# First x blocks on a second DMA queue, the first four layer norms cut between units, and key features joined later

## The chip, the cores and the metric

The kernel runs on one core of one Trainium2 chip. The metric is the device time of one execution in microseconds (us), as the median of several executions. Profiles come from one execution each; "span" is the profiled time, about 1.7 to 1.9 us shorter than the metric of the same execution.

## The reference

Two layers, each used twice on x of 2048 x 1024 in bf16: linear attention with 32 heads, and a gated ReGLU block with inner width 3584. Layer norm stands before each.

```python
    def _A_ref(x, wqkv, wo):
        ...                                  # q, k, v = x @ wqkv, 32 heads of 32
        phi = lambda t: jnp.where(t > 0, t + 1, jnp.exp(t)) + 1e-6
        pq, pk = phi(q), phi(k)
        kv = jnp.einsum("bhsd,bhse->bhde", pk, v)
        ...                                  # num / den, then @ wo
    x = A_x
    x = x + _A_ref(_layernorm(x, axis=-1), A_wqkv, A_wo)
    x = x + _B_ref(_layernorm(x, axis=-1), B_W_gate, B_W_up, B_W_down)
    ...                                      # the same two once more
```

## The kernel before

x is kept as 16 blocks of 128 rows. In the first attention layer, a *unit* is one block times 512 columns of a weight: eight matmuls of 128x512 into one of four PSUM buffers. A key unit (columns k0 or k1) then goes through `phi`: ACT takes the Exp, DVE clamps it (`min` 1, plus 1e-6), and DVE joins it with max(x, 0) and so gives the PSUM buffer back. `later.at(n, f)` runs f after n further units. In the head (the first quarter of layer 0) the program fixes the order of DVE and ACT itself. In the kernel before it does so in two separate lists, the norms of blocks 0 to 3 and the units; in the changed kernel both stand in one list.

```python
    def head(self):
        ...                                  # 10 matmuls on a zero block, to warm TensorE up
        self.load_x(0, 0)                    # all on SyncE's queue
        self.load_x(0, 1)
        k0(0, H)
        self.load_x(1)
        k0(H, 2 * H)
        self.load_x(2)
        k1()
        self.load_x(3)
        ...
            for j in range(QT):              # blocks 0 to 3, one after the other
                for c in range(2):
                    self.ln_stat(j, src[j], c, stats[j])
                r = self.ln_rstd(stats[j])
                xn = self.xn_home(0, j)
                for h in (0, 1) if j == 0 else (None,):
                    self.ln_scale(src[j], *r, xn, h)
                for h in range(2):
                    turn(j, xn, h)           # 4 transposes, then a copy out of PSUM

    def phi(self, ps, out, kind):
        e = self.ep.tile([P, NW], F32, tag="e")
        if kind == "v":
            nc.scalar.activation(out=e, in_=ps, func=ACT.Exp)
            nc.vector.tensor_scalar(out=e, in0=e, scalar1=1.0, scalar2=1e-6, op0=ALU.min,
                                    op1=ALU.add)           # the clamp
        ...
        def join():
            nc.vector.scalar_tensor_tensor(out=out, in0=ps, scalar=0.0, in1=e,
                                           op0=ALU.max, op1=ALU.add)
        if self.phi_lag:                     # 2 in the head
            self.later.at(self.phi_lag, join)
```

Of the kernel before, what the change touches and what calls it, by code (L numbers as in the profile page):

```python
# [7 lines left out]
ALU = mybir.AluOpType  # L8
ACT = mybir.ActivationFunctionType
# [3 lines left out]
P = 128  # L13
NW = 512
HD = 32
QT = 4
LNLAG = 1
ZR = 5
NZ = 11
Z3 = 3  # L20
PHILAG = 2
KINDS = (("vvss", "vvss"), ("vvss", "vvss"))


class _Ring:
# [59 lines left out]
class _Net:  # L85
# [135 lines left out]
    def head(self):  # L221

        nc, tc, ring = self.nc, self.tc, self.ring
        H = self.KT // 2

        zero = self.ep.tile([P, NW], BF16, tag="e")
        nc.vector.memset(zero, 0.0)
        idle = self.ps3.tile([P, NW], F32, tag="b")
        for _ in range(10):
            nc.tensor.matmul(idle, lhsT=zero[:, 0:P], rhs=zero, start=True, stop=True)  # L230

        k0, k1, v0, q0, q1 = (ring.place() for _ in range(5))
        self.load_x(0, 0)
        self.load_x(0, 1)
        k0(0, H)
        self.load_x(1)
        k0(H, 2 * H)
        self.load_x(2)
        k1()
        self.load_x(3)  # L240
        q0()
        self.load_x(4)
        self.load_x(5)
        self.load_x(6)
        self.load_x(7)
        q1()
        for t in range(8, self.ST):
            self.load_x(t)
        v0()
        src = self.xb  # L250
        self.xnT[0, 0] = self.xnTp.tile([P, self.KT, QT * P], BF16, tag="xnT", name="xnT0_0")
        stats = [self.small.tile([P, 2, nc.vector.BN_STATS_DIM], F32, tag="stats", name=f"st{j}")
                 for j in range(QT)]

        def turn(j, xn, h):
            tp = self.ps3.tile([P, H, P], BF16, tag="b")
            for i in range(H):
                kt = h * H + i
                nc.tensor.transpose(tp[:, i, :], xn[:, kt * P:(kt + 1) * P], self.ident)
            dst = self.xnT[0, 0][:, h * H:(h + 1) * H, j * P:(j + 1) * P]  # L260
            if h == 0:
                nc.vector.tensor_copy(out=dst, in_=tp)
            else:
                nc.scalar.activation(out=dst, in_=tp, func=ACT.Copy)

        with tc.manual_schedule(engines={mybir.EngineType.DVE, mybir.EngineType.Activation}):
            for j in range(QT):
                for c in range(2):
                    self.ln_stat(j, src[j], c, stats[j])
                r = self.ln_rstd(stats[j])  # L270
                xn = self.xn_home(0, j)
                for h in (0, 1) if j == 0 else (None,):
                    self.ln_scale(src[j], *r, xn, h)
                for h in range(2):
                    turn(j, xn, h)

    def ln_turn(self, layer, t, xn):
        nc = self.nc
# [6 lines left out]
    def ln_at(self, delay, layer, t, lag):  # L285
        def stat():
            scale = self.ln_norm(layer, t)
            self.later.at(LNLAG, lambda: norm(scale))

        def norm(scale):  # L290
            xn = scale()
            self.later.at(lag, lambda: self.ln_turn(layer, t, xn))

        self.later.at(delay, stat)
# [5 lines left out]
    def phi(self, ps, out, kind):  # L300

        nc = self.nc
        e = self.ep.tile([P, NW], F32, tag="e")
        if kind == "v":
            nc.scalar.activation(out=e, in_=ps, func=ACT.Exp)
            nc.vector.tensor_scalar(out=e, in0=e, scalar1=1.0, scalar2=1e-6, op0=ALU.min,  # L306
                                    op1=ALU.add)
        else:
            nc.scalar.activation(out=e, in_=ps, func=ACT.Relu, scale=-1.0)
            nc.scalar.activation(out=e, in_=e, func=ACT.Exp, scale=-1.0)  # L310
            if kind == "s":
                nc.scalar.activation(out=e, in_=e, func=ACT.Identity, bias=self.eps6[:, 0:1])  # L312
            else:
                nc.gpsimd.tensor_tensor(out=e, in0=e, in1=self.eps6[:, 0:1].to_broadcast([P, NW]),
                                        op=ALU.add)
        def join():
            nc.vector.scalar_tensor_tensor(out=out, in0=ps, scalar=0.0, in1=e,  # L317
                                           op0=ALU.max, op1=ALU.add)

        if self.phi_lag:  # L320
            self.later.at(self.phi_lag, join)
        else:
            join()

    def load_x(self, t, c=None):
        D = self.D
        lo, hi = (0, D) if c is None else (c * D // 2, (c + 1) * D // 2)
        self.nc.sync.dma_start(out=self.xb[t][:, lo:hi], in_=self.x_v[:, t, lo:hi])


    def plan_A(self, l):
# [9 lines left out]
    def layer_A(self, l, last_ln):  # L341
        nc, G, KT, D = self.nc, self.G, self.KT, self.D
        ring, later = self.ring, self.later
# [5 lines left out]
        zrow = self.kvc.tile([P, D], BF16, tag="zrow")  # L349
        ksum = self.prodp.tile([P, D], F32, tag="prod", name=f"ksum{l}")  # L350

        def project(name, l_q, j):
            w = ring.get((l, name))
            ps = self.ps.tile([P, NW], F32, tag="a")
            for kt in range(KT):
                nc.tensor.matmul(ps, lhsT=self.xnT[l, l_q][:, kt, j * P:(j + 1) * P],  # L356
                                 rhs=w[:, kt, :], start=(kt == 0), stop=(kt == KT - 1))
            return ps

        def k_unit(q, j, c):  # L360
            t = q * QT + j
            pk = self.pk_home(l, t)
            self.phi(project(f"k{c}", q, j), pk[:, c * NW:(c + 1) * NW], KINDS[l // 2][min(q, 1)][c])
            later.at(1 + (10 if self.phi_lag else 0), lambda: k_sum(t, slice(c * NW, (c + 1) * NW)))

        def k_sum(t, cols):
# [54 lines left out]
        def q_unit(sc, j, c, lag=None):  # L421
            if c == 0 and (sc, j) not in pq_of:
                if sc < self.NQ - 1:
                    a = self.xnTp.tile([P, QT, D], BF16, tag="xnT", name=f"pq{l}_{sc}")
                    for i in range(QT):
                        pq_of[sc, i] = a[:, i, :]
                else:
                    pq_of[sc, j] = self.xnp.tile([P, D], BF16, tag="xn", name=f"pq{l}_{sc}_{j}")
            pq = pq_of[sc, j]
            self.phi(project(f"q{c}", sc, j), pq[:, c * NW:(c + 1) * NW], KINDS[l // 2][min(sc, 1)][2 + c] if sc < 3 else "v")  # L430
            if c == H - 1 and lag is not None:
                later.at(lag, lambda: z_mult(sc, j))

# [50 lines left out]
        def column_major(f, q):  # L484
            return [lambda j=j, c=c: f(q, j, c) for c in range(H) for j in range(QT)]
# [11 lines left out]
                        later.tick()  # L497

        if l == 0:
            self.head()  # L500
        else:
            ring.free_before((l, "k0"))
        for i in range(QT, self.ST):
            self.ln_at((4 if l == 0 else 2) + 3 * (i - QT), l, i, 2)
        first = column_major(k_unit, 0)
        if l == 0:

            first = [first[c * QT + j] for c, j in ((0, 0), (0, 1), (1, 0), (0, 2), (1, 1), (1, 2),
                                                    (0, 3), (1, 3))]

        def quarter0():
            self.phi_lag = PHILAG if l == 0 else 0
            run(first)
            run(column_major(q_unit, 0))
            later.at(1, lambda: None)
            self.phi_lag = 0
# [9 lines left out]
        run(row_major(k_unit, self.NQ - 1))  # L526
        with self.tc.manual_schedule(engines={mybir.EngineType.DVE, mybir.EngineType.Pool}):
            ring.free_before((l, "v0"))
            later.at(ZR, z_row)
            for i in range(NZ):  # L530
                later.at(ZR + 2 + 2 * i, lambda i=i: z_mult(*divmod(i, QT)))
            for d in range(KT):
                m_units(d)
            if l > 0:
                later.at(1, lambda: [self.bring_back(t) for t in range(self.NS)])
            q3 = row_major(q_unit, self.NQ - 1)
            out0 = column_major(out_unit, 0)

            def with_fold(u, i):
                return lambda: (u(), fold_wo(2 * i), fold_wo(2 * i + 1))  # L540

            run(q3[:3])
            run([with_fold(u, i) for i, u in enumerate(q3[3:] + out0[:3])])
            ring.free_slowly((l, "o0"), later, 2)
            for i in range(NZ, self.ST):
                later.at(1 + Z3 * (i - NZ), lambda i=i: z_mult(*divmod(i, QT)))
            run(out0[3:])
            self.ln_later(last_ln, 0, 5, 4, 3)
            for sc in range(1, self.NQ):
                run(row_major(out_unit, sc))  # L550
# [132 lines left out]
```

## Time and profile before

| | before |
|---|---|
| median of 4 executions | 1635.45 us (1635.25 to 1636.06) |
| profiled span | 1634.0 us |
| PE idle in the first 44.6 us | 6.6 us |
| second half of k0 / k1 landed (completion records) | 8.98 / 12.66 us |

This is the view of groups by shape, limited to 10 to 32 us; after the count come busy time, mean ns of one, and idle time of the engine just before it with its releaser.

```profile
L306 DVE TENSOR_SCALAR e<-e 128x512 f32<-128x512 f32 x8 | 5.9, 733 | 2.6 <-ACT e L305 2.5
```

For 2.5 us DVE stood in front of a clamp whose Exp was not ready. The longest of these waits, 1.47 us, stands ahead of a copy of transposed x whose transposes had ended at 10.49 us, and PE waits for that copy until 11.53:

```profile
10.71 0.43 DVE L306 TENSOR_SCALAR e<-e 128x512 f32<-128x512 f32 x1 [1.47 <-ACT e L305]
11.05 0.42 DVE L262 COPY xnT<-tp 128x512 bf16<-128x512 bf16 x1
```

### The profile page before, as it was taken

To read this page: it belongs to the slowest core of one execution; us is meant where nothing else is said; L and a number is where in the kernel's file an instruction comes from. 1 tells how busy PE (TensorE), PEld (TensorE's weight loads), DVE (VectorE), ACT (ScalarE), POOL (GpSimd) and SP (SyncE) were. 2 spreads that over 40 slices of the span, in tenths; PEclk is the share of its full clock that TensorE was granted. 3 is DMA by queue.
4 is the path that set the end of the run, shared out by engine and by line. 5 is a ranking of instruction groups with operands and counts; after the bars stand their busy time and mean duration, and the time that the engine had idled before them with its cause. 6 is when DMAs were issued, how large, how long until landed. Compare 5 with 4: busy or idle time off the path is not lost.

```text
span 1634.0 us, 18308 instructions
## 1 busy us (share of the span) xinstructions
PE 1616.6 (99%) x7506; PEld 742.7 (45%) x7658; DVE 571.6 (35%) x947; ACT 331.9 (20%) x635; POOL 201.8 (12%) x134
## 2 busy tenths in 40 slices
PE   8999999999999999999999999999999999999999
PEld 3444444444444444444444444444444444444444
DVE  7855585223112321222165547941122111211211
ACT  5841202101110110111067312121011101101110
POOL 2349230000000000000023592100000000000000
PEclk9999999999999999999999999999999999999999
DMA  8313547458445544444550147474554454454452
GB/s 251 59 52 52 174 74 188 146 165 232 154 139 175 175 151 158 160 150 141 168 129 1 52 91 251 79 198 145 177 162 149 156 191 155 145 162 157 155 161 72
DMA packets 298245, 235.05 MB, mean 144 GB/s; under 512 B 101296, under 2 KB 294192, under 8 KB 298160
## 3 DMA queue, kind: packets, MB, share of 16 engines
q1 hardware_dynamic: 293408, 229.66, 47.3%
q10 hardware_dynamic: 4752, 4.20, 0.8%
q8 instruction: 60, 0.98, 0.2%
q14 instruction: 25, 0.20, 0.0%
HBM read 201.33 MB, written 8.39 MB: 128 GB/s over the span
## 4 chain that ended last, share of the span: by engine, by line
PE 97%; DVE 1%; ACT 1%; issue 1%; DMA 0%; SPq 0%
PE pu L582 24%; PE pg L582 24%; PE acc L606 23%; PE ps L356 12%; PE ps L473 7%; PE ps L390 7%; PE kv L403 0%; PE fold L461 0%; DMA t<-in_A_wqkv_dram 0%; PE acc_last L606 0%; DVE e L306 0%; DVE stats L148 0%; DVE slab L317 0%; ACT e L310 0%; DVE st L148 0%
## 5 line engine op out<-in xcount | busy, mean ns | idle before, releaser
L582 PEld LDWEIGHTS <-t 128*128 128x128 bf16 x3584 | 350.7, 98 | 422.9
L582 PE MATMUL pu<-xnT,t 128*128 128x512 bf16 x1757 | 420.2, 379 | 1.9
L582 PE MATMUL pg<-xnT,t 128*128 128x512 bf16 x1756 | 419.8, 379 | 1.8
L606 PE MATMUL acc<-t,hT 128*128 128x512 bf16 x1727 | 380.6, 379 | 1.9
L588 DVE TENSOR_TENSOR hT<-pu,rg 128x512 bf16<-128x512 f32 x224 | 154.7, 691 | 572.8 <-PE pu L582 553.4
L587 ACT ACTIVATE rg<-pg 128x512 f32<-128x512 f32 x224 | 133.5, 596 | 737.3 <-PE pg L582 665.9
L606 PEld LDWEIGHTS <-hT 128*128 128x128 bf16 x1820 | 178.1, 98 | 209.0
L356 PE MATMUL ps<-t,xnT 128*128 128x512 bf16 x1002 | 223.3, 379 | 5.5 <-DVE slab L317 1.4
L356 PEld LDWEIGHTS <-xnT 128*128 128x128 bf16 x1024 | 99.8, 98 | 125.1 <-issue 4.7
L473 PE MATMUL ps<-T,pqT 128*128 128x512 bf16 x502 | 111.3, 379 | 0.5
L155 ACT ACTIVATE rstd<-mv,eps 128x1 f32<-128x1 f32 x64 | 18.8, 294 | 333.3 <-DVE mv L153 333.3
L623 DVE TENSOR_TENSOR xo<-x,acc 128x512 bf16<-128x512 f32 x31 | 21.3, 687 | 170.3 <-PE acc L606 170.3
L436 POOL TENSOR_TENSOR prod<-pq,zrow 128x1024 f32<-128x1024 bf16 x32 | 68.1, 2127 | 87.8 <-DVE den L441 75.6
L148 DVE BATCH_NORM_STATS2 stats<-x 128x6 f32<-128x512 f32 (+1 forms) x120 | 78.1, 673 | 0.8
L473 PEld LDWEIGHTS <-pqT 128*128 128x128 bf16 x512 | 50.1, 98 | 60.4
L370 POOL CAST ksum<-x 128x512 f32<-128x512 bf16 x2 | 1.7, 867 | 605.4 <-DVE x L317 605.4
L620 DVE TENSOR_TENSOR x<-x,acc 128x512 f32<-128x512 f32 x32 | 21.6, 674 | 138.5 <-PE acc L606 137.4
L372 POOL TENSOR_TENSOR ksum<-ksum,slab 128x512 f32<-128x512 f32 x46 | 54.2, 1184 | 84.9 <-DVE slab L317 75.3
L317 DVE SCALAR_TENSOR_TENSOR pq<-ps,e 128x512 bf16<-128x512 f32 x64 | 43.9, 688 | 58.6 <-ACT e L312 58.0
L448 POOL TENSOR_TENSOR pq<-pq,den 128x1024 bf16<-128x1024 bf16 x32 | 61.8, 1938 | 3.1 <-DVE den L443 3.1
L441 DVE TENSOR_REDUCE den<-prod 128x32 f32<-128x1024 f32 x32 | 38.9, 1217 | 52.6 <-POOL prod L436 52.6
L390 PE MATMUL ps<-slab,x 128*128 128x512 bf16 x250 | 56.1, 379 | 0.3
(58 smaller groups left out, 607.2 us busy)
## 6 DMA issues: line engine op xcount, KB each, us to landing
t<-in_B_W_gate_dram SPq DMA_DIRECT2D x56, 1024.0 KB, 6.7
t<-in_B_W_up_dram SPq DMA_DIRECT2D x56, 1024.0 KB, 5.2
t<-in_B_W_down_dram SPq DMA_DIRECT2D x64, 896.0 KB, 5.0
t<-in_A_wqkv_dram SPq DMA_DIRECT2D x11, 1024.0 KB, 6.2
t<-in_A_wo_dram SPq DMA_DIRECT2D x4, 1024.0 KB, 6.4
away<-x SPq DMA_DIRECT2D x8, 512.0 KB, 4.0
x<-away SPq DMA_DIRECT2D x8, 512.0 KB, 7.3
out_dram<-xo ACTq DMA_DIRECT2D x31, 128.0 KB, 2.1
```

Of the source, the lines that this page charges most:

```text
L148: self.nc.vector.bn_stats(out=stats[:, c, :], in_=src[:, c * fmax:(c + 1) * fmax])
L317: nc.vector.scalar_tensor_tensor(out=out, in0=ps, scalar=0.0, in1=e, op0=ALU.max, op1=ALU.add)
L356: nc.tensor.matmul(ps, lhsT=self.xnT[l, l_q][:, kt, j * P:(j + 1) * P], rhs=w[:, kt, :], start=(kt == 0), stop=(kt == KT - 1))
L372: nc.gpsimd.tensor_tensor(out=ksum[:, cols], in0=ksum[:, cols], in1=pk, op=ALU.add)
L390: nc.tensor.matmul(ps, lhsT=self.xn[l, t][:, d * P:(d + 1) * P], rhs=self.pk[l, t][:, h * NW:(h + 1) * NW], start=(t == 0), stop=(t == sel ...
L436: nc.gpsimd.tensor_tensor(out=prod, in0=pq_of[sc, j], in1=zrow, op=ALU.mult)
L448: nc.gpsimd.tensor_tensor(out=heads(pq), in0=heads(pq), in1=den[:, :].unsqueeze(2).to_broadcast([P, D // HD, HD]), op=ALU.mult)
L473: nc.tensor.matmul(ps, lhsT=pqT[sc][:, g, j * P:(j + 1) * P], rhs=T[g // 2][:, g % 2, n2 * NW:(n2 + 1) * NW], start=(g == 0), stop=(g == G ...
L582: nc.tensor.matmul(ps, lhsT=w[:, kt, fi * P:(fi + 1) * P], rhs=self.xnT[l, q][:, kt, :], start=(kt == 0), stop=(kt == KT - 1))
L587: nc.scalar.activation(out=rg, in_=pg, func=ACT.Relu)
L588: nc.vector.tensor_tensor(out=h[:, fi, :], in0=pu, in1=rg, op=ALU.mult)
L606: nc.tensor.matmul(ps[:, 0:n], lhsT=hT[ft // 4][:, ft % 4, j * P:(j + 1) * P], rhs=wd[:, k, i * n:(i + 1) * n], start=(ft == 0), stop=(ft ...
```

## The change

The intent is to bring x and the first weights side by side, to cut the norms of blocks 0 to 3 so that they fill the time between units, and to move the joins of the key units away from the units that produce them. The constants that became literals change nothing and are left out here.

```diff
-        self.load_x(0, 0)
+        self.load_x(0, 0, nc.scalar)
         self.load_x(0, 1)
+        self.load_x(1, None, nc.scalar)
         k0(0, H)
-        self.load_x(1)
+        self.load_x(2, None, nc.scalar)
         k0(H, 2 * H)
-        self.load_x(2)
+        self.load_x(3, None, nc.scalar)
         k1()
-        self.load_x(3)
 ...
+        def block0():
+            stat(0, 0)
+            stat(0, 1)
+            rstd(0)
+            stat(1, 0)
+            scale(0, 0)
+            scale(0, 1)
+            t0 = turn(0, 0)
+            t1 = turn(0, 1)
+            t0("s")
+            stat(1, 1)
+            rstd(1)
+            t1("v")
+            k(0, 0, between)      # block 1's scales and 4 transposes between its 6th and 7th matmul
 ...
+        def block(j, c, n):       # scale and transposes of block n, stats of n + 1, unit (j, c)
+            scale(n)
+            t0 = turn(n, 0)
+            t1 = turn(n, 1)
+            t0("s")
+            t1("s")
+            if n + 1 < QT:
+                norm(n + 1)
+            k(j, c)
 ...
             nc.scalar.activation(out=e, in_=ps, func=ACT.Exp)
-            nc.vector.tensor_scalar(out=e, in0=e, scalar1=1.0, scalar2=1e-6, op0=ALU.min,
-                                    op1=ALU.add)
 ...
         def join():
+            if kind == "v":
+                nc.vector.tensor_scalar(out=e, in0=e, scalar1=1.0, scalar2=1e-6, op0=ALU.min,
+                                        op1=ALU.add)
             nc.vector.scalar_tensor_tensor(out=out, in0=ps, scalar=0.0, in1=e,
                                            op0=ALU.max, op1=ALU.add)
 ...
-            self.ln_at((4 if l == 0 else 2) + 3 * (i - QT), l, i, 2)
+            self.ln_at((8 if l == 0 else 2) + 3 * (i - QT), l, i, 2)
 ...
-            self.phi_lag = PHILAG if l == 0 else 0        # PHILAG = 2
+            self.phi_lag = 3 if l == 0 else 0
```

More of the change, by code (lines that the diff above doesn't have):

```diff
@@ L16 @@
 QT = 4
-LNLAG = 1
-ZR = 5
-NZ = 11
-Z3 = 3
-PHILAG = 2
-KINDS = (("vvss", "vvss"), ("vvss", "vvss"))
 class _Ring:
@@ L253, in head, with stat, rstd, scale @@
                  for j in range(QT)]
-        def turn(j, xn, h):
+        rs, xn = {}, {}
+        def stat(j, c):
+            self.ln_stat(j, src[j], c, stats[j])
+        def rstd(j):
+            rs[j] = self.ln_rstd(stats[j])
+            xn[j] = self.xn_home(0, j)
+        def scale(j, h=None):
+            self.ln_scale(src[j], *rs[j], xn[j], h)
+        def turn(j, h):
             tp = self.ps3.tile([P, H, P], BF16, tag="b")
@@ L258, in turn, with take, head_units, between @@
                 kt = h * H + i
-                nc.tensor.transpose(tp[:, i, :], xn[:, kt * P:(kt + 1) * P], self.ident)
+                nc.tensor.transpose(tp[:, i, :], xn[j][:, kt * P:(kt + 1) * P], self.ident)
             dst = self.xnT[0, 0][:, h * H:(h + 1) * H, j * P:(j + 1) * P]
-            if h == 0:
-                nc.vector.tensor_copy(out=dst, in_=tp)
-            else:
-                nc.scalar.activation(out=dst, in_=tp, func=ACT.Copy)
-        with tc.manual_schedule(engines={mybir.EngineType.DVE, mybir.EngineType.Activation}):
-            for j in range(QT):
-                for c in range(2):
-                    self.ln_stat(j, src[j], c, stats[j])
-                r = self.ln_rstd(stats[j])
-                xn = self.xn_home(0, j)
-                for h in (0, 1) if j == 0 else (None,):
-                    self.ln_scale(src[j], *r, xn, h)
-                for h in range(2):
-                    turn(j, xn, h)
+            def take(engine):
+                if engine == "v":
+                    nc.vector.tensor_copy(out=dst, in_=tp)
+                else:
+                    nc.scalar.activation(out=dst, in_=tp, func=ACT.Copy)
+            return take
+        return stat, rstd, scale, turn
+    def head_units(self, k, stat, rstd, scale, turn):
+        def block0():
[12 more added lines that the diff above has]
+            k(0, 0, between)
+        def between():
+            scale(1, 0)
+            t0 = turn(1, 0)
+            scale(1, 1)
+            t0("v")
+        def block1():
+            turn(1, 1)("v")
+            norm(2)
+            k(1, 0)
+        def norm(j):
+            stat(j, 0)
+            stat(j, 1)
+            rstd(j)
+        def block(j, c, n):
[7 more added lines that the diff above has]
+            k(j, c)
+        return [block0, block1, lambda: k(0, 1), lambda: block(1, 1, 2), lambda: k(2, 0),
+                lambda: block(2, 1, 3), lambda: k(3, 0), lambda: k(3, 1)]
     def ln_turn(self, layer, t, xn):
@@ L287, in stat @@
             scale = self.ln_norm(layer, t)
-            self.later.at(LNLAG, lambda: norm(scale))
+            self.later.at(1, lambda: norm(scale))
         def norm(scale):
@@ L310, in phi @@
             nc.scalar.activation(out=e, in_=e, func=ACT.Exp, scale=-1.0)
-            if kind == "s":
-                nc.scalar.activation(out=e, in_=e, func=ACT.Identity, bias=self.eps6[:, 0:1])
-            else:
-                nc.gpsimd.tensor_tensor(out=e, in0=e, in1=self.eps6[:, 0:1].to_broadcast([P, NW]),
-                                        op=ALU.add)
+            nc.scalar.activation(out=e, in_=e, func=ACT.Identity, bias=self.eps6[:, 0:1])
         def join():
+            if kind == "v":
+                nc.vector.tensor_scalar(out=e, in0=e, scalar1=1.0, scalar2=1e-6, op0=ALU.min,
+                                        op1=ALU.add)
             nc.vector.scalar_tensor_tensor(out=out, in0=ps, scalar=0.0, in1=e,
@@ L323, in phi, with load_x @@
             join()
-    def load_x(self, t, c=None):
+    def load_x(self, t, c=None, queue=None):
         D = self.D
         lo, hi = (0, D) if c is None else (c * D // 2, (c + 1) * D // 2)
-        self.nc.sync.dma_start(out=self.xb[t][:, lo:hi], in_=self.x_v[:, t, lo:hi])
+        (queue or self.nc.sync).dma_start(out=self.xb[t][:, lo:hi], in_=self.x_v[:, t, lo:hi])
     def plan_A(self, l):
@@ L350, in layer_A, with project @@
         ksum = self.prodp.tile([P, D], F32, tag="prod", name=f"ksum{l}")
-        def project(name, l_q, j):
+        def project(name, l_q, j, between=None):
             w = ring.get((l, name))
@@ L355, in project @@
             for kt in range(KT):
+                if between and kt == KT - 2:
+                    between()
                 nc.tensor.matmul(ps, lhsT=self.xnT[l, l_q][:, kt, j * P:(j + 1) * P],
@@ L358, in project, with k_unit @@
             return ps
-        def k_unit(q, j, c):
+        def k_unit(q, j, c, between=None):
             t = q * QT + j
             pk = self.pk_home(l, t)
-            self.phi(project(f"k{c}", q, j), pk[:, c * NW:(c + 1) * NW], KINDS[l // 2][min(q, 1)][c])
+            self.phi(project(f"k{c}", q, j, between), pk[:, c * NW:(c + 1) * NW], "v")
             later.at(1 + (10 if self.phi_lag else 0), lambda: k_sum(t, slice(c * NW, (c + 1) * NW)))
@@ L429, in q_unit @@
             pq = pq_of[sc, j]
-            self.phi(project(f"q{c}", sc, j), pq[:, c * NW:(c + 1) * NW], KINDS[l // 2][min(sc, 1)][2 + c] if sc < 3 else "v")
+            self.phi(project(f"q{c}", sc, j), pq[:, c * NW:(c + 1) * NW], "s" if sc < self.NQ - 1 else "v")
             if c == H - 1 and lag is not None:
@@ L499, in layer_A @@
         if l == 0:
-            self.head()
+            steps = self.head()
         else:
@@ L503, in layer_A @@
         for i in range(QT, self.ST):
-            self.ln_at((4 if l == 0 else 2) + 3 * (i - QT), l, i, 2)
-        first = column_major(k_unit, 0)
+            self.ln_at((8 if l == 0 else 2) + 3 * (i - QT), l, i, 2)
         if l == 0:
-            first = [first[c * QT + j] for c, j in ((0, 0), (0, 1), (1, 0), (0, 2), (1, 1), (1, 2),
-                                                    (0, 3), (1, 3))]
+            first = self.head_units(lambda *a: k_unit(0, *a), *steps)
+        else:
+            first = column_major(k_unit, 0)
         def quarter0():
-            self.phi_lag = PHILAG if l == 0 else 0
+            self.phi_lag = 3 if l == 0 else 0
             run(first)
@@ L528, in layer_A @@
             ring.free_before((l, "v0"))
-            later.at(ZR, z_row)
-            for i in range(NZ):
-                later.at(ZR + 2 + 2 * i, lambda i=i: z_mult(*divmod(i, QT)))
+            later.at(5, z_row)
+            for i in range(11):
+                later.at(7 + 2 * i, lambda i=i: z_mult(*divmod(i, QT)))
             for d in range(KT):
@@ L544, in layer_A @@
             ring.free_slowly((l, "o0"), later, 2)
-            for i in range(NZ, self.ST):
-                later.at(1 + Z3 * (i - NZ), lambda i=i: z_mult(*divmod(i, QT)))
+            for i in range(11, self.ST):
+                later.at(1 + 3 * (i - 11), lambda i=i: z_mult(*divmod(i, QT)))
             run(out0[3:])
```

## The prediction

> **What bounds the kernel now.** The page first: busy shares, then the chain that ended last.
>
> ```profile
> PE 1616.6 (99%) x7506; PEld 742.7 (45%) x7658; DVE 571.6 (35%) x947; ACT 331.9 (20%) x635; POOL 201.8 (12%) x134
> ...
> PE 97%; DVE 1%; ACT 1%; issue 1%; DMA 0%; SPq 0%
> ```
>
> TensorE (PE) sets the end: 1616.6 of 1634.0 us are matmul, so only 17.4 us could be won by any reordering. The next question is where these stand. Busy time by stretches (length, then PE, weight loads, DVE, ACT, POOL with counts, clock, DMA share, GB/s):
>
> ```profile
> 0.00:44.60 44.60, 38.01 (x184) 17.07 (x188) 34.32 (x74) 25.96 (x53) 9.56 (x14) 1.00 0.78 236
> 44.60:60.00 15.40, 15.29 (x70) 7.03 (x72) 15.33 (x33) 13.19 (x30) 4.80 (x4) 1.00 0.42 70
> 60.00:1600.00 1540.00, 1532.42 (x7088) 702.07 (x7231) 516.28 (x833) 292.73 (x553) 187.42 (x116) 1.00 0.48 144
> ```
>
> The first 44.6 us hold 6.6 us of the idle time. Later it is a short pause of about 0.05 us per 10.8 us, which no part of the change touches. So I read the head alone, in the timeline of PE (start, length, work, and in brackets the idle time before it and its releaser):
>
> ```profile
> 5.82 0.61 PE L259 MATMUL tp<-ident,x 128*128 128x128 bf16 x8
> 6.72 1.04 PE L356 MATMUL ps<-t,xnT 128*128 128x512 bf16 x4 [0.30 <-DVE xnT L262]
> 9.02 1.02 PE L356 MATMUL ps<-t,xnT 128*128 128x512 bf16 x4 [1.26 <-DMA t<-in_A_wqkv_dram]
> 9.88 0.61 PE L259 MATMUL tp<-ident,x 128*128 128x128 bf16 x8
> 11.53 2.55 PE L356 MATMUL ps<-t,xnT 128*128 128x512 bf16 x11 [1.04 <-DVE xnT L262]
> 14.11 0.62 PE L259 MATMUL tp<-ident,x 128*128 128x128 bf16 x8
> ...
> 21.91 3.61 PE L356 MATMUL ps<-t,xnT 128*128 128x512 bf16 x15 [0.41 <-DVE slab L317]
> 25.82 1.89 PE L356 MATMUL ps<-t,xnT 128*128 128x512 bf16 x8 [0.29 <-DVE slab L317]
> 28.14 1.89 PE L356 MATMUL ps<-t,xnT 128*128 128x512 bf16 x8 [0.44 <-DVE slab L317]
> 30.32 13.97 PE L356 MATMUL ps<-t,xnT 128*128 128x512 bf16 x63 [0.30 <-DVE slab L317]
> ```
>
> There are two kinds of gap. Up to 11.53 PE waits for the first weights and for transposed x. From 21.91 it waits for "slab", the DVE instruction that joins a unit's features and gives its PSUM buffer back (four buffers, so unit n+4 waits for the join of unit n); one more such wait, of 0.28 us, ends at 44.58. A bracket understates the loss: a 512-column matmul is drawn 0.38 us long but follows its neighbour after 0.2155 us in a full stream, so a gap after one costs the bracket plus 0.16.
>
> DVE is the reason for the second kind. In 13.4 to 21.9 us it is busy 8.23 of 8.50 us, and its order is the cause: the norm of block 4 and the clamp of a unit (L306) stand before joins that PE needs.
>
> ```profile
> 17.01 0.64 DVE L317 SCALAR_TENSOR_TENSOR slab<-ps,e 128x512 bf16<-128x512 f32 x1
> 17.69 0.55 DVE L164 TENSOR_SCALAR x<-x,mv,rstd 128x1024 bf16<-128x1024 bf16 x1
> 18.20 1.33 DVE L306 TENSOR_SCALAR e<-e 128x512 f32<-128x512 f32 x1
> 19.46 0.68 DVE L148 BATCH_NORM_STATS2 stats<-x 128x6 f32<-128x512 bf16 x1
> 20.06 0.40 DVE L262 COPY xnT<-tp 128x512 bf16<-128x512 bf16 x1
> 20.38 0.68 DVE L148 BATCH_NORM_STATS2 stats<-x 128x6 f32<-128x512 bf16 x1
> 21.09 0.21 DVE L153 BATCH_NORM_AGGREGATE mv<-stats 128x2 f32<-128x12 f32 x1
> 21.22 0.64 DVE L317 SCALAR_TENSOR_TENSOR slab<-ps,e 128x512 bf16<-128x512 f32 x1
> ```
>
> The join of 21.22 releases PE at 21.91; ahead of it stand 1.6 us of block 4's norm (two stats and the aggregate at 0.68, 0.68 and 0.21).
>
> **What the Trainium skill says.** "DMA: Bandwidth & Descriptors", section "Issuing engines are not separate DMA queues": DMAs started from different engines run on the same 16 DMA engines, and a second issuer saves sequencer time only. "Perfetto Trace Analysis", section "DMA Instruction — HWDGE (DVE, Sync)": the descriptor generator is locked for one DMA at a time, so the saving may be smaller still. The trace has SyncE issues of 0.40 to 0.51 us each, the first seven end to end from 0.74 to 4.2 us; no second queue is active there, so sharing is not shown. "ScalarE: Activation LUTs", section "What ACT_TABLE_LOAD costs": about 1283 ns for a table load, an ACT instruction; the trace has 1.28 us from 0.73. The new x issues stand directly behind it. "SBUF — State Buffer", section "Who interferes with whom": a DVE tensor_scalar in a two-port mode and a GpSimd instruction shut each other out. The trace agrees: L306 takes 0.43 us alone, and 1.06 to 1.37 us the three times it meets a 1.2 us POOL add.
>
> **The change, part by part.** No work is removed. Block 1's scale is split (0.74 us in two pieces against 0.55 in one, L164), and one of eight xnT copies goes from DVE to ACT. PE has the same 15,318 instructions in both orders, and the constants that became literals change nothing: key units still have kind v, query units kind s. What moves:
>
> (1) *x blocks 0 (half), 1, 2, 3 on the ScalarE queue.* Before, one queue brought, by the completion records: first half of k0 5.78, x1 6.45, second half of k0 8.98, x2 9.69, k1 12.66, x3 13.37 us. That is 3,072 KB, with some 350 KB/us in the later part. In the new order k0 and k1 stand one behind the other on SyncE while x1 to x3 compete from the side. The second half of k0 then lands between 8.98 (x costs it nothing) and 8.98 + 512 KB / 360 KB per us = 10.4 (x2 and x3 pass it first); I take 9.7. For k1 the bytes ahead are all 3,072 KB, so at most 13.4, less what two issuers win at the start: I take 12.7. x1 lands at 4.5 to 6.5; x2 and x3 stop mattering.
>
> (2) *Norms of blocks 0 to 3 in pieces.* The DVE order now has the first stats of block 1 before block 0's scale, so the first transposes wait for x1: x1's landing plus 0.61 (stats), two scales and the hops, so 6 to 7.5 us against 5.82. That is hidden as long as four matmuls (0.86 us) end before the second half of k0, at 9.7. From there: 4 more matmuls of unit (0,0), 8 transposes between them and 8 matmuls of (1,0), so 12 x 0.2155 + 8 x 0.056 = 3.03, and k1 is needed at 12.8. Before, that point (first matmul on k1) was at 11.53 + 8 x 0.2155 = 13.25. Gain 0.45 us, with k0 anywhere from 8.98 (then k1 decides) to 10.4 (a loss of 0.25).
>
> (3) *Joins three units later, with the clamp beside the join; other norms from tick 8, not 4.* After 13.25 the kernel before still lost: 0.20 before the transposes at 14.11 (a 0.41 us step against 0.2155), and the brackets 0.41 + 0.29 + 0.44 + 0.30 + 0.28 = 1.72 plus 5 x 0.16 = 0.80. Sum 2.72 us. To see what is left I walked the new order of each engine with the durations of the rows above (join 0.61 to the next start, clamp 0.36 or until the POOL add ends, stats 0.61, scale 0.46; ACT 0.49 to 0.62). The same walk through the old order gives the trace's gaps, each within 0.3 us. In the new one every join ends 1.7 us or more before unit n+4 needs the buffer, up to the first query units, since block 4's stats stand behind five joins; 0.3 to 0.4 us of small waits stay, near 43 us, where keys of block 4 meet the last query joins. Gain 2.72 - 0.35 = 2.4 us.
>
> Sum 0.45 + 2.4 = 2.85 us, nothing after 60 us: 1635.3 - 2.8 = 1632.5.
>
> **Rivals.** *(a) Weights starved.* If x takes more than its share, or ScalarE's issues slow SyncE's, the second half of k0 lands at 10.4 or later and k1 at 13.5 to 14. Part (2) turns into a loss of 0.3 to 0.8, total gain 1.6 to 2.1: 1633.2 to 1633.7. For it: the DMA is already near its top (350 GB/s in 6.7 to 13.4 us) and bytes are not reduced. Against it: before 6.7 us only 206 GB/s moved, room that a second issuer can fill.
> *(b) The table load holds the x issues back* to 2.0 us, so half of x0 lands near 4.0 instead of 3.0 and x1 a little later. In the walk PE starts its transposes some 0.6 us later, hidden before k0's second half: about 1632.5 too. Only x1 after 8.5 us would cost.
> *(c) The clamps beside the joins all meet the POOL adds* that each join releases, 0.9 us each. The walk has two such meetings, against three before; with 1.7 us of slack it would take several in a row. If so, half of part (3) is lost: 1633.8.
> *(d) Loads run better*, k0 near 8.5 and k1 near 11.7: part (2) gains up to 1.5, total 3.9: 1631.4.
>
> **Range and chances.** Part (3) is the firm term (1.9 to 2.5), part (2) the loose one (-0.5 to +1.3); together 1.5 to 3.8 us, widened a little at the top for the chip's own spread: 1631.4 to 1634.0. Two per cent is 32.7 us, more than all idle time of PE (17.4), so faster by 2% can't be; slower by 2% would need a stall in every later stage, which this change doesn't touch.
>
> **What would show it.** Right: the brackets "<-DVE slab" between 21 and 31 us are gone; PE idle in the first 44.6 us falls from 6.6 to about 3.8; the first matmul on k1 at 12.8 +- 0.7; matmuls steady from about 13 to 43 us; the second half of k0 lands at 9.2 to 10.4; the first transposes start at 6 to 7.5. Wrong: an ACT issue after 2 us with PE waiting for x; new waits for weights over 2 us; L306 mostly over 1 us with "slab" waits still there; or any new gap after 60 us, for instance at transposes of blocks 4 to 7, whose norms start four units later.

## The result, and the profile after

The changed kernel takes 1632.51 us (1632.31 to 1632.99, 4 executions), against 1635.45 before: 2.94 us less. The ratio is 0.9982, with a 95% interval of 0.9965 to 0.9999. Ratios here are the mean time of one kernel's runs over that of the other's in the same rounds, so they are not quite the ratio of the quoted medians.

Busy time by stretches of the changed kernel, same columns as before:

```profile
0.00:44.60 44.60, 41.55 (x200) 18.89 (x201) 35.75 (x80) 28.72 (x62) 9.83 (x15) 1.00 0.79 236
60.00:1600.00 1540.00, 1540.00 (x7232) 702.06 (x7231) 514.48 (x829) 291.46 (x551) 186.31 (x116) 1.00 0.49 144
```

PE's idle time in the first 44.6 us falls from 6.59 to 3.05 us (about 3.8 was predicted). That is more than the time gained, in part because matmuls at the slow clock count as busy: warm-up and first transposes are drawn 4.45 and 1.06 us long here, 3.89 and 0.61 before. The second line corrects a reading of the prediction, and is taken up below. The timeline of PE in the head:

```profile
2.10 4.45 PE L224 MATMUL idle<-zero 128*128 128x512 bf16 x10 [2.10 <-DVE zero L221]
6.34 1.06 PE L264 MATMUL tp<-ident,x 128*128 128x128 bf16 x8
7.66 1.24 PE L403 MATMUL ps<-t,xnT 128*128 128x512 bf16 x4 [0.26 <-ACT xnT L271]
9.48 0.59 PE L403 MATMUL ps<-t,xnT 128*128 128x512 bf16 x2 [0.58 <-DMA t<-in_A_wqkv_dram]
...
10.81 3.63 PE L403 MATMUL ps<-t,xnT 128*128 128x512 bf16 x16
...
18.91 43.37 PE L403 MATMUL ps<-t,xnT 128*128 128x512 bf16 x198
```

From 9.5 us on there is no bracket: none of the waits for "slab" is left, and only one short wait for the second half of k0 remains. The transposes took 1.06 us for eight, against 0.61 before; the clock is why (see below). The DVE lines that answer to those of before, from the third join (which stood at 21.22 us before) to block 4's norm:

```profile
17.14 0.69 DVE L362 SCALAR_TENSOR_TENSOR slab<-ps,e 128x512 bf16<-128x512 f32 x1
...
19.79 0.42 DVE L360 TENSOR_SCALAR e<-e 128x512 f32<-128x512 f32 x1
20.24 0.69 DVE L362 SCALAR_TENSOR_TENSOR slab<-ps,e 128x512 bf16<-128x512 f32 x1
20.85 1.27 DVE L142 BATCH_NORM_STATS2 stats<-x 128x6 f32<-128x512 bf16 x2
22.16 0.21 DVE L147 BATCH_NORM_AGGREGATE mv<-stats 128x2 f32<-128x12 f32 x1
22.29 0.37 DVE L360 TENSOR_SCALAR e<-e 128x512 f32<-128x512 f32 x1
22.69 0.69 DVE L362 SCALAR_TENSOR_TENSOR slab<-ps,e 128x512 bf16<-128x512 f32 x1
```

Clamp and join follow each other, and block 4's stats come behind five joins instead of ahead of the third. The clamp's group in 10 to 32 us:

```profile
L360 DVE TENSOR_SCALAR e<-e 128x512 f32<-128x512 f32 x8 | 3.6, 451 | 0.0
```

The wait of 2.5 us for the Exp is gone, and the mean clamp is 451 ns instead of 733, since it meets fewer POOL adds: one clamp here takes 0.82 us, where three took 1.06 to 1.37 before.

**Where the time came from.** The weight loads of PE are recorded completely in both traces (7,658 each), so the start of the n-th one shows by how much the changed kernel leads. In both the 43rd is the first of a k1 unit; it stands at 12.34 against 13.05 us: a lead of 0.72. At the 131st, about 29 us, the lead is 2.77, and at the 501st as at the 7,001st it is 2.75. So some 0.7 us come from the start and 2.03 from the stretch after it, up to 29 us, where the waits for the joins had stood; the head's last waits are as large in both (0.44 us at 44.6 before, 0.27 at 43 and 0.18 at 57 after), and nothing comes from after 60 us.

### The profile page after: what moved, and what is told of

The parts are those of the page before. It is cut to its first block, busy times and chain, and to the rows that moved or that the text cites. A ratio compares the mean times of both kernels' runs of the same rounds, so it can differ in the third digit from the quotient of the medians.

```text
span 1631.2 us, 18462 instructions
## 1 busy us (share of the span) xinstructions
PE 1625.2 (100%) x7658; PEld 743.1 (46%) x7658; DVE 570.8 (35%) x947; ACT 331.2 (20%) x636; POOL 201.5 (12%) x134
## 4 chain that ended last, share of the span: by engine, by line
PE 98%; ACT 1%; DMA 0%; DVE 0%; issue 0%; SPq 0%
PE pu L628 24%; PE pg L628 24%; PE acc L652 23%; PE ps L403 12%; PE ps L520 7%; PE ps L437 7%; DMA t<-in_A_wqkv_dram 0%; PE kv L450 0%; PE fold L508 0%; PE acc_last L652 0%; ACT e L355 0%; ACT e L354 0%; ACT e L356 0%; PE tp L264 0%; DVE pq L362 0%
```

## The experiments

Five timed executions each; "faster" compares medians with the kernel before (1635.79, 1635.30 and 1635.25 us). For seven of the twelve the five times all lie clearly on one side of the kernel before and the 95% interval of the ratio leaves out 1. For the change without the second queue, join and late norms alone, and the clamp alone, the interval just reaches 1 (upper ends 1.0003, 1.0004 and 1.0001), though their five times all lie below all nine of the kernel before; for the second queue alone and the early norms the times overlap with it. The last two columns read the profile as just described: the lead at the first k1 unit, and what is added from there to the 501st weight load.

| run | faster by, us | lead at k1 | added after |
|---|---|---|---|
| second queue alone, on the kernel before | -0.08 | -0.11 | -0.01 |
| change without the second queue | 1.36 | -0.66 | 2.00 |
| the same with 13 warm-up matmuls | 2.43 | 0.10 | 2.03 |
| join and late norms alone, on the kernel before | 1.43 | -0.43 | 1.29 |
| clamp beside its join alone, on the kernel before | 1.99 | 0.54 | 1.93 |
| change, join two units on | 3.49 | 1.44 | 2.05 |
| change, clamp back behind the Exp | -2.39 | 0.58 | -1.78 |
| change, norms of blocks 4 on from tick 4 | 0.72 | 1.32 | 0.02 |
| change, x3 behind k1 | 3.14 | 1.55 | 2.03 |
| change once more | 2.78 | 1.33 | 2.03 |
| x3 behind k1, join two units on | 2.92 | 1.87 | 2.08 |
| the same, warm-up earlier | 3.36 | 1.63 | 2.08 |

The "lead at k1" is that of one execution and moves by 0.6 us between two profiles of the same kernel (0.72 and 1.33 for the changed one), while "added after" was 2.03 in both. Where the number of warm-up matmuls differs, the weight loads are counted from after the warm-up. No edit gives a wrong result; all twelve agree with the reference.

### Is it the queue? The second queue alone

```diff
 # kernel before
-        self.load_x(0, 0)
+        self.load_x(0, 0, nc.scalar)
 ...                               # x1 to x3 likewise, as in the change
```

> The kernel before, with only the load order of the changed kernel: x0's first half and x1 to x3 on the ScalarE queue. Theory T (the gain is in the order of DVE, the queue gives nothing by itself): the second half of k0 lands near 9.4 instead of 8.98 us because x2 and x3 share the way, the joins still hold TensorE up at 21 to 31 us; 0.2 to 0.6 us slower than before. Rival Q (the second queue brings the data earlier and that is the gain): 1 to 2.5 us faster.

Measured: 1635.87 us, 0.08 slower, ratio 1.0 (0.9987 to 1.0014). The second queue alone is worth nothing: all five waits of the old head are there again, 0.12 us later. The loss is smaller than theory T said, as the second half of k0 landed at 9.10 us and not at 9.4.

### The change without the second queue, and the clock

```diff
 # changed kernel: loads as before, all on SyncE
-        self.load_x(0, 0, nc.scalar)
+        self.load_x(0, 0)
 ...
```

> The changed kernel with all loads back on SyncE in the old order. T: x1 lands near 6.45, so the first transposes start near 7.5 us, but TensorE still gets the second half of k0 at 9.0 and k1 at 12.7; 2.5 to 3.2 us faster than before, as the changed kernel (2.75 in the profile). Q: at most 1.5 us faster than before.

Measured: 1634.43 us, 1.36 faster than before. T's number was wrong and Q's fits, though the joins gave their full 2.00 us. The loss is in the first unit. Four executions took 1634.4 to 1634.5 us, with a mean granted clock of 0.999 in three of them, and one took 1633.12. The profile is one of the slow ones:

```profile
2.10 4.45 PE L224 MATMUL idle<-zero 128*128 128x512 bf16 x10 [2.10 <-DVE zero L221]
7.26 1.03 PE L264 MATMUL tp<-ident,x 128*128 128x128 bf16 x8 [0.72 <-DVE x L158]
8.56 2.74 PE L403 MATMUL ps<-t,xnT 128*128 128x512 bf16 x6 [0.26 <-ACT xnT L271]
```

Six matmuls took 2.74 us, that is 0.43 each, twice the 0.2155 of the later ones: TensorE still ran at half clock. x1 had landed at 6.17 us instead of 5.12, so PE stood idle for 0.72 us behind the warm-up, and the trace's record of the granted clock has full speed only from 11.5 us on. The Trainium skill, "TensorE: Matmul & The Clock Gate", section "What's actually happening", says that the clock is released after a busy window of about 3.4 us, and that these windows run freely, not from the kernel's start. The full-clock stretch that the traces record lasts 1628.16, 1624.74 or, in this run, 1621.33 us, so it grows or shrinks in steps of 3.4 us. Matmuls start at 2.1 us in every profile but that of the earlier warm-up, and the full clock comes at 5.3 us before, at 8.1 and 6.4 in two profiles of the changed kernel, and at 5.1 to 8.1 wherever a time was recorded, but at 11.5 in this run, the one with the gap. (In three profiles it comes 3.0 to 3.3 us after the first matmul, a little less than a whole window.) That the gap is the reason is an inference from one profile so far. So the next run kept PE busy:

```diff
 # change without the second queue
-        for _ in range(10):
+        for _ in range(13):
```

> The one-queue form of the changed kernel with 13 warm-up matmuls for 10, so that TensorE stays busy until x1 is in. In the profile of the one-queue form the full clock was granted only at 11.5 us, after an idle gap of 0.72 us at the end of the warm-up, and its one fast run of five took 1633.12. Theory C (the second queue's worth is mainly that x1 comes before the warm-up ends, so the clock is granted in time): full clock by 8.5 us in the profile, 2.0 to 3.0 us faster than before, 0.7 to 1.5 faster than the one-queue form. Rival X (x1's later landing itself holds the first unit up): no gain over the one-queue form, about 1.4 us faster than before.

Measured: 1632.87 us, 2.43 faster than before, as theory C said. Three more matmuls of warm-up gave 1.07 us (2.43 less 1.36) of the 1.42 that leaving out the queue had cost (2.78 of the changed kernel's repeat less 1.36; the three come from three calls).

```profile
2.09 4.71 PE L224 MATMUL idle<-zero 128*128 128x512 bf16 x13 [2.09 <-DVE zero L221]
8.13 0.72 PE L264 MATMUL tp<-ident,x 128*128 128x128 bf16 x8 [1.33 <-DVE x L158]
9.22 1.47 PE L403 MATMUL ps<-t,xnT 128*128 128x512 bf16 x6 [0.36 <-ACT xnT L271]
```

The six matmuls take 1.47 us although x was later still (x1 at 7.05). In this one profile the window happened to close early (full clock at 5.6 us, before the 13 were through), and it is of one of the two slower executions (1633.59), so the profile alone does not prove the edit; the times do better, as none of the five is near 1634.4 (1632.73 to 1633.66). The rival, that x1's later landing itself holds the first unit up, has this against it: even with x1 still later, this profile lies 0.8 us below the last one. That it was the clock is likely, and not shown in a trace. What remains of the queue's worth, 0.35 us, is within the differences between calls.

### Join and late norms alone

```diff
 # kernel before: clamp into join() as in the change, and
-PHILAG = 2
+PHILAG = 3
-            self.ln_at((4 if l == 0 else 2) + 3 * (i - QT), l, i, 2)
+            self.ln_at((8 if l == 0 else 2) + 3 * (i - QT), l, i, 2)
```

> The kernel before, with its own head and one queue, and only part (3): join and clamp together three units later, other norms from tick 8. T, from the walk: the waits for slab at 21 to 31 us shrink to one of 0.5 us near 15; 1.6 to 2.2 us faster than before, most of the whole gain. If the pieces in the head are what matters: under 0.8 us faster.

Measured: 1634.36 us, 1.43 faster, just under the range. The waits for "slab" are gone, but with the old head two gaps take their place, at 16.5 us for the copy of transposed x and at 19.7 us for block 3's scale, both late on DVE: it adds 1.29 us after k1, not 2.03.

### Two units or three

```diff
 # changed kernel
-            self.phi_lag = 3 if l == 0 else 0
+            self.phi_lag = 2 if l == 0 else 0
```

> The changed kernel with the join (clamp beside it) two units on, not three. If the third unit of delay is what frees DVE: 1 us or more slower than the changed kernel. If the place of the clamp, next to its join and no longer right behind the Exp, is what frees it (the walk's answer): within 0.3 us of the changed kernel, that is 2.4 to 3.0 us faster than before.

Measured: 1632.30 us, 3.49 faster than before; the changed kernel has 1632.51 and 1632.47. It adds 2.05 us after k1 against 2.03. The third unit of delay is worth nothing.

### The clamp's place

```diff
 # changed kernel: clamp back, join still three units on
             nc.scalar.activation(out=e, in_=ps, func=ACT.Exp)
+            nc.vector.tensor_scalar(out=e, in0=e, scalar1=1.0, scalar2=1e-6, op0=ALU.min,
+                                    op1=ALU.add)
 ...
         def join():
-            if kind == "v":
-                nc.vector.tensor_scalar(...)
```

> The changed kernel with the clamp back where it was, issued with its unit right behind the Exp, and the join alone three units later. Walk: DVE, in order, then stands before each clamp until TensorE has finished that unit and ACT its Exp, while norms and joins wait behind it; 1 to 2 us slower than before, so 4 us slower than the changed kernel. If the place of the clamp did not matter and only the join's did: as the changed kernel, 2.5 to 3 us faster than before.

Measured: 1637.69 us, 2.39 slower than before and about 5 slower than the change: a little more than the walk gave. After the first k1 unit the two profiles differ by 3.81 us (2.03 and -1.78), close to the walk's 4; the rest lies at the start, where the trace puts a wait of 0.64 us, up to 11.82, down to weights that landed at 11.78. The clamp's group in 10 to 32 us:

```profile
L353 DVE TENSOR_SCALAR e<-e 128x512 f32<-128x512 f32 x8 | 4.5, 564 | 7.0 <-ACT e L352 7.0
```

DVE waits 7.0 us in front of clamps, and PE then waits for joins and for transposed x. The counterpart on the kernel before moves only this one instruction in the program:

```diff
 # kernel before
             nc.scalar.activation(out=e, in_=ps, func=ACT.Exp)
-            nc.vector.tensor_scalar(out=e, in0=e, scalar1=1.0, scalar2=1e-6, op0=ALU.min,
-                                    op1=ALU.add)
 ...
         def join():
+            if kind == "v":
+                nc.vector.tensor_scalar(out=e, in0=e, scalar1=1.0, scalar2=1e-6, op0=ALU.min,
+                                        op1=ALU.add)
```

> The kernel before with one thing moved: the clamp stands beside its join (still two units on), head, loads and norms as before. If the clamp's place is the larger part of the joins' gain, as the walk says: 1.1 to 1.7 us faster than before. If it only works together with the three units and the late norms: under 0.6 us.

Measured: 1633.26 us, 1.99 faster; the changed kernel in the same call is 2.78 faster. It beat its range (1.1 to 1.7).

```profile
L316 DVE TENSOR_SCALAR e<-e 128x512 f32<-128x512 f32 x8 | 4.2, 528 | 0.8 <-ACT e L305 0.7
```

DVE waits 0.7 us for the Exp instead of 2.5, and all the brackets "<-DVE slab" of PE are gone. One instruction moved in the program is some 70% of the gain (1.99 of 2.78). In the trace more has moved, since the order between the list of norms and the list of units is not written: the first clamp runs at 10.05 us and its join at 12.04, with a copy and two stats between them. And block 4's two stats (16.56 and 17.26) still run ahead of the third join, which nevertheless comes at 18.81 and not at 21.22. So block 4's norm, ahead of that join in both, did not by itself hold it up.

### The late norms

```diff
 # changed kernel
-            self.ln_at((8 if l == 0 else 2) + 3 * (i - QT), l, i, 2)
+            self.ln_at((4 if l == 0 else 2) + 3 * (i - QT), l, i, 2)
```

> The changed kernel with the norms of blocks 4 and on starting at tick 4 again. Walk: waits of 0.4 to 0.5 us come back near 18 to 22 us and one of 0.6 near 41; 1.3 to 1.9 us faster than before, so about 1.2 us slower than the changed kernel. If the late start of these norms is not what matters: 2.5 us or more faster than before.

Measured: 1634.58 us, 0.72 faster than before, so about 2 us of the change lost: more than the walk's 1.2. Block 4's norm pushes block 3's scale back, and its transposes come late:

```profile
20.46 0.62 PE L264 MATMUL tp<-ident,x 128*128 128x128 bf16 x8 [0.71 <-DVE x L158]
```

With the new head the late start is needed; with the old head and the clamp moved, the early norms did no such harm (1.93 us added after k1). These two parts do not add up independently.

### Further on: x3 behind k1, and an earlier warm-up

```diff
 # changed kernel
-        self.load_x(3, None, nc.scalar)
         k1()
+        self.load_x(3)
```

> The changed kernel with x3 taken from the ScalarE queue and put behind k1 on SyncE, since block 3 is needed last. If the second half of k0 is what holds the first unit: it lands near 8.8 instead of 9.44 us, k1 near 11.8 instead of 12.45, and all that follows moves up; 3.2 to 4.0 us faster than before, 0.4 to 0.9 faster than the changed kernel. If the DMA engines' share is not what sets it, or x3 then holds DVE: no gain over the changed kernel.

Measured: 1632.16 us, 3.14 faster than before, under the range. The second half of k0 landed at 8.06 and k1 at 11.07 us, earlier than expected, yet the first unit's matmuls started only at 7.77 and ended behind it: k0 no longer decides; by the order of DVE it is x1 (landed at 5.60), whose first stats stand ahead of block 0's scale, and the trace puts the wait before the first transposes down to that scale (0.22 us, at 6.68). A gain over the changed kernel of 0.3 us is suggested, not shown. It was run at another time.

```diff
 # x3 behind k1, and
-            self.phi_lag = 3 if l == 0 else 0
+            self.phi_lag = 2 if l == 0 else 0
```

> The changed kernel with x3 behind k1 on SyncE and the join two units on. The two single edits measured 3.14 and 3.49 us faster than before, each in its own call. If both are real and independent: 3.6 to 4.2 faster than before, 0.5 or more faster than the changed kernel in this call. If the second was only a lucky landing of the weights: as x3 behind k1 alone, 3.0 to 3.5.

Measured: 1632.33 us, 2.92 faster, below both ranges; 0.14 better than the changed kernel, which is not told from nothing. So a gain of its own behind the 3.49 of "two units" is not confirmed.

```diff
 # the same, the zero block first of all memsets, and
-        for _ in range(10):
+        for _ in range(12):
```

> As the last, and the zero block of the warm-up is set first of all DVE memsets, with 12 warm-up matmuls for 10: TensorE starts near 1.1 instead of 2.1 us. Theory C: the full clock comes before the first transposes in most runs, so these take 0.06 and not 0.11 us each and the first four matmuls 0.22 and not 0.43; with the second half of k0 near 8.1 that is worth 0.2 to 0.8 us more. If k0's landing alone sets the first unit: no gain.

Measured: 1631.89 us (1631.76 to 1632.08), 3.36 faster than before, 0.44 faster than the last run (whose five, 1631.88 to 1632.35, overlap with these) and 0.58 faster than the changed kernel, whose five runs (1632.38 to 1632.76) all lie above it. This version is the fastest, by 0.04% over the changed kernel. Its profile had the full clock at 6.9 us, after the first transposes had begun at 6.38, so the mechanism that was expected is not what that one profile shows; whether the 0.44 us are real, and their cause, stays open.

> The changed kernel once more, as the measure for the other three of this call and for the spread between profiles of one kernel. All theories: 2.6 to 3.4 us faster than before; in the profile the second half of k0 anywhere from 8.4 to 9.5 us and the full clock anywhere from 5 to 8.5 us.

The changed kernel again: 1632.47 us, 2.78 faster; second half of k0 at 8.83 us, full clock at 6.4. All as expected.

## Why the prediction was right

The time (1632.5 predicted, 1632.51 measured) and the two parts' order were right; that the sum agrees to 0.01 us is luck, since the two terms missed in opposite directions. Two of its signs held only in one of the two profiles of the changed kernel: the second half of k0 landed at 9.44 and 8.83 us (9.2 to 10.4 said), and the first matmul on k1 stood at 12.55 and 11.94 (12.8 +- 0.7). By its steps:

- **PE sets the end, and only the head matters.** Right: the lead at the 501st weight load is that of the end. Its bound of 17.4 us was wrong, though. What was read as "a short pause of about 0.05 us per 10.8 us" is missing records: before, the page counts 7,506 matmuls and 7,658 weight loads, after, 7,658 of both, and PE's idle time after 60 us is zero while the lead does not move. (Its 15,318 instructions of PE are 15,316 by the weight loads and matmuls of the complete trace; nothing rests on it.) One group of both pages shows it:

```profile
L582 PE MATMUL pu<-xnT,t 128*128 128x512 bf16 x1757 | 420.2, 379 | 1.9
```

```profile
L628 PE MATMUL pu<-xnT,t 128*128 128x512 bf16 x1792 | 423.3, 379 | 0.0
```

- **Part (1), the loads.** The sizes failed. "I take 9.7" for the second half of k0 was too late: over the six profiles with x1 to x3 on ScalarE it landed at 8.72 to 9.44, mean 8.95, and over the five on one queue at 8.24 to 9.41, mean 8.79. x passing from the side cost the weights 0.16 us by these means, not 0.7, and with such spreads that is not told from nothing. k1 landed at 11.7 to 12.5 (12.7 predicted), mean 11.90, against 11.95 to 13.10, mean 12.48, on one queue. The rate shows why. Stretches of the kernel before, then of the changed one, GB/s last:

```profile
3.00:5.50 2.50, 2.50 (x8) 0.92 (x7) 1.83 (x5) 0.50 (x2) 0.00 (x0) 1.00 0.91 302
5.50:8.00 2.50, 1.96 (x15) 0.94 (x13) 2.13 (x6) 0.60 (x1) 0.00 (x0) 1.00 0.98 290
```

```profile
3.00:5.50 2.50, 2.50 (x8) 0.85 (x7) 1.86 (x4) 0.30 (x2) 0.00 (x0) 1.00 1.06 377
5.50:8.00 2.50, 2.24 (x12) 1.16 (x11) 2.21 (x6) 1.16 (x4) 0.00 (x0) 1.00 1.05 369
```

  From 3 to 8 us the rate was 367 to 375 GB/s in all nine profiles with x on ScalarE, and 296 to 329 in all five on one queue: a fifth more by the means. That is rival (d), in part. From 8 to 12 us the nine are a little lower (349 to 355 against 360 to 368).
- **Part (2), gain 0.45.** The lead at the first k1 unit was 0.72 and 1.33 us in two profiles, so 0.45 was too small, from the late landing alone: with the measured landing of the second half of k0 in place of 9.7, the prediction's sum gives 0.71 and 1.32, and 1.43 and 1.31 for the variants with two units and with early norms, where the traces have 1.44 and 1.32. The mechanism held; its input was off. It stops holding where k0 lands near 8 (x3 behind k1: 2.09 by the sum, 1.55 in the trace). A term was missing altogether: the clock. In the first profile transposes and the first matmul ran at half speed until 8.1 us, hidden only because k0 came at 9.44; where x came late it was not hidden and the time was over 1 us longer.
- **Part (3), gain 2.4.** It measured 2.03 in both profiles of the changed kernel, and 2.00 to 2.08 in all variants that kept it; the term was 0.37 us too large. What failed is the 0.35 us of small waits left over: they are 0.72 us, namely 0.10 and 0.17 before the transposes at 14.4 and 18.5 us, 0.27 at 43 and 0.18 at 57 us (steps between matmul starts, less 0.2155), and 2.72 - 0.72 = 2.00. The errors of (2) and (3) have opposite signs, which is why the sum is nearly exact. The cause was named too widely: "Joins three units later" is not needed (two give the same); the clamp's place is, alone worth 1.99 us on the old kernel. And the late norms, which the prediction had as relief for the joins, protect the transposes of block 3; the norm of block 4, named there beside the clamp as the cause, still stood ahead of the third join when the clamp alone was moved, and PE did not wait.
- **Rivals.** (a) did not come. (b) did not come: the x issues run beside the table load. Nor did the two issuers hold each other up at first, as the prediction thought possible: the first four issues on each run in pairs, 0.40 to 0.52 us each, no longer than on one queue (0.40 to 0.51).

```profile
0.73 1.28 ACT L677 ACT_TABLE_LOAD   x1 [0.73 <-PEq L713]
0.76 1.97 ACTq L373 DMA_DIRECT2D x<-in_A_x_dram  x4
```

  (c) did not come: the clamps met fewer POOL adds than before, mean 451 against 733 ns.

## What to carry to other kernels

On an engine that runs in order, put an instruction where its input is surely ready, beside its consumer, and not right behind its producer: one clamp moved in this way gave some two thirds of this gain, and moved back in the changed kernel it cost 5 us. Then look in the trace whether the order came out as meant. At the start of a kernel, see that TensorE has no gap between warm-up and first work before the full clock is granted; here a gap of 0.72 us went with a loss of about 1 us, most of which three more warm-up matmuls took back. And before idle time in a profile is counted as winnable, compare the counts of matmuls and weight loads: where matmul records are missing, the idle time is not there.

## What the Trainium skill lacked or had wrong

- "DMA: Bandwidth & Descriptors", "Issuing engines are not separate DMA queues": says that a second issuer only saves issue time, which is usually small. At this start it was not small: from 3 to 8 us the rate was 367 to 375 GB/s with two issuers against 296 to 329 with one. The last issue of the head's x began at 2.2 us instead of 4.2; whether saved issue time is all of it was not tested. In the profiles x1 landed at 5.1 to 5.6 us instead of 6.0 to 7.1.
- No page says whether a DMA issue on ScalarE waits for a table load ahead of it. It did not: first issue at 0.76 us, the load from 0.73 to 2.01.
- "ScalarE: Activation LUTs", "Terms", gives about 2.7 us for a table load, and does not say there that this includes a drain; the trace has 1.28 us for the load, as the page's own section "What ACT_TABLE_LOAD costs" says.
- "TensorE: Matmul & The Clock Gate", "What's actually happening": gives the transition a variation of 500 ns either way (and further down, without a time, says that the same kernel can run 6, 11 or 14 slow matmuls). Here the full clock came 3.0 to 6.0 us after the first matmul in twelve profiles, a spread of 3 us, and 9.4 us after it in the one with a gap of 0.72 us.
